# Random-feature attention and a feed-forward layer on one core: attention's matmuls in plain float32, each head on half of the array

## The chip, the cores and the metric

The kernel runs on one core of a Trainium2 chip. The metric is the device time of one execution in microseconds; less is better. The core's engines work side by side, each with its own queue of instructions: TensorE (PE; its weight loads are listed apart as PEld), VectorE (DVE), ScalarE (ACT), GpSimd (POOL) and SyncE (SP), which issues most of the transfers.

## The reference

There are 8 batches, 8 heads, 576 tokens, a head size of 64, 128 features and a hidden size of 2048, all in float32.

```python
scale = 1.0 / np.sqrt(np.sqrt(D))
q_s, k_s = q * scale, k * scale
def phi(x):
    h = x @ omega.T - sum(x * x) / 2          # 64 -> 128 features
    h = h - max(h over features)
    return exp(h) / sqrt(128)
q_p, k_p = phi(q_s), phi(k_s)
kv = einsum('bhsm,bhsd->bhmd', k_p, v)        # sums over the tokens
z = sum(k_p over the tokens)
out = (q_p @ kv) / (q_p @ z + 1e-6)
x = out as (8 * 576, 512)
h = x @ w_in                                  # 512 -> 2048
result = (h - tanh(h)) @ w_out                # 2048 -> 512
```

The term sum(x * x) / 2 and the factor 1 / sqrt(128) fall away: the maximum is subtracted, and the quotient has the rest on both sides.

## The kernel before

**Layout.** Queries and keys lie transposed in memory, two heads in one tensor: partitions 0 to 63 hold the head dimensions of head 0 of a pair, partitions 64 to 127 those of head 1. There are four pairs (`c`). The 4608 tokens are cut into 18 chunks (`ch`) of 256 for queries and for the feed-forward part; keys go by batch (`b`) of 576 tokens, four tiles of 128 and a last one of 64. A pair's two last tiles of 64 share one tile.

**Units.** `k_unit(b, c)` makes, for a batch and a pair, the sums kv and z; `q_unit(ch, c)` makes the attention of a chunk and a pair and leaves it in `xh` and `xl` (`x_split`), the operand of the feed-forward part. Both are generators; `tick` starts new ones by a table of start times (`start`) and carries each one a step further. Between steps come the feed-forward steps `ffn_h` (hidden, tanh) and `ffn_out` (output sums), with a `beat` of attention after each. The instructions' order on each engine follows from the order of issue and from the scheduler's own timing model (`schedule_with_timeline_sim=True`).

**Two formats.** A plain float32 matmul is one call and shows as two pairs of weight load and matmul in the trace. The feed-forward part, and attention from batch 2 and chunk 3 on, split each operand into a high and a low part of the format float32r, which shows as one load and one matmul for each call.

**First stage (`native=True`), batches 0 and 1 and chunks 0 to 2.** Attention is in plain float32 over all 128 rows. `features_f` (L153) multiplies a token tile of both heads with `om_bd`, omega for both heads on a block diagonal, 256 columns. The values carry a column of ones (width E = 66), so the sum over the tokens gives kv and z at once (L201, L205); the last, shared tile is spread over block diagonals `kd` and `vd` by POOL copies (L184, L185). z is brought to all partitions by two transposes (L221). kv is held for both heads on a block diagonal `kvf`, so the numerators of two heads add up in one accumulator (L374). In this stage the feed-forward weights are also fetched and decoded (`fetch`, `decode`: ACT, DVE and POOL work on 16 weight blocks), and the first feed-forward steps begin.

**Steady stage (`native=False`), the rest.** `split_rows` (ACT L75, DVE L129 and L130) puts the high part of a head in 64 rows and its low part in the other 64. `features` (L132) multiplies with `om2`, omega's high and low part side by side, 256 columns; ACT copies one half (L143), DVE adds the other and finds the minimum (L146), ACT takes the exponentials (L150). `k_single` (L227) splits features and values (POOL L250 and L258, DVE L249 and L259), sums them on TensorE (L266), adds up z on POOL (`zsum`, L271 and L272, L289, L290), and brings kv and z into place with two transposes and two multiplications with ones (L302, L304). `q_unit` divides the features by the denominators (DVE L347, L350, L359), transposes them (L366), splits them (ACT L389, DVE L390), multiplies with the split kv (L396, L397), and adds the halves (ACT L400 and L401, DVE L402 and L403).

**PSUM.** Its eight banks have tags (`pj0`, `pj1`, `pk`, `pt`, `po0`, `po1`, `h0`, `h1`). `h0` and `h1` belong to the hidden layer, `po0` and `po1` to the output. `mode` says which tags projections (`pj`), sums (`pk`) and transposes and numerators (`pt`) rotate through. A two-head projection lies in one bank.

**Order around the change.** SP issues the loads, in the first stage in program order (`chain=True`), and each engine works through its queue in order.

Of the kernel before, what the change touches and what calls it, by code (L numbers as in the profile page):

```python
# [8 lines left out]
F32 = mybir.dt.float32  # L9
# [10 lines left out]
P = 128  # L20
# [3 lines left out]
TC = 256  # L24
# [7 lines left out]
def favor_attention_ffn(ctx: ExitStack, tc: tile.TileContext, qT, kT, va, vt, omT, w, out):  # L32
# [63 lines left out]
    omf = a0.tile([P, M], F32, name="omf")  # L96
# [7 lines left out]
    om2 = om.rearrange("p a m -> p (a m)")  # L104

    om_bd = a0.tile([P, 2, M], F32, name="om_bd")
    nc.gpsimd.memset(om_bd, 0.0)
    nc.gpsimd.tensor_scalar(om_bd[0:D, 0], omf[0:D], -SCALE, 1.0, op0=ALU.mult, op1=ALU.mult)
    nc.gpsimd.tensor_scalar(om_bd[D:P, 1], omf[D:P], -SCALE, 1.0, op0=ALU.mult, op1=ALU.mult)

    oms = a0.tile([P, M], F32, name="oms")
    nc.gpsimd.tensor_scalar(oms, omf, -SCALE, 1.0, op0=ALU.mult, op1=ALU.mult)

    def kv_tiles(pool, names):

        ts = [(pool.tile([P, 9, E], F32, name=f"v{i}"), pool.tile([P, P], F32, name=f"kd{i}"),
               pool.tile([P, 2, E], F32, name=f"vd{i}")) for i in names]
        for v, kd, vd in ts:
            for x in (kd, vd):
                nc.gpsimd.memset(x, 0.0)  # L120
            nc.gpsimd.memset(v[:, :, D:], 1.0)
        return ts


    def split_rows(x, f):

        copy(mode["hi"], x[0:D, 0, :], f[0:D])
        copy(mode["hi"], x[D:P, 1, :], f[D:P])
        nc.vector.tensor_sub(x[D:P, 0, :], f[0:D], x[0:D, 0, :].bitcast(F32))  # L129
        nc.vector.tensor_sub(x[0:D, 1, :], f[D:P], x[D:P, 1, :].bitcast(F32))  # L130

    def features(lhs, name):  # L132

        n = len(lhs)
        ph = att("phi", [P, 4, M], F32, f"phi_{name}")
        nb = sb.tile([P, 4], F32, tag="nb", name=f"nb_{name}", bufs=12)

        for g in range(0, n, 2):
            m = min(2, n - g)
            pj = ps.tile([P, 2, 2 * M], F32, tag=bank("pj"), name=f"pj_{name}_{g}")  # L140
            for i in range(m):
                nc.tensor.matmul(pj[:, i], lhs[g + i], om2, start=True, stop=True)  # L142
            nc.scalar.copy(ph[:, g : g + m], pj[:, :m, M:])  # L143
            for i in range(m):
                j = g + i
                nc.vector.tensor_tensor_reduce(  # L146
                    ph[:, j], pj[:, i, :M], ph[:, j], scale=-SCALE, scalar=3.0e38,
                    op0=ALU.add, op1=ALU.min, accum_out=nb[:, j : j + 1])
        for j in range(n):
            nc.scalar.activation(ph[:, j], ph[:, j], AF.Exp, bias=nb[:, j : j + 1], scale=-1.0)  # L150
        return ph

    def features_f(f, toks, name):  # L153

        n = 2 * len(toks)
        ph = att("phi", [P, 4, M], F32, f"phi_{name}")
        nb = sb.tile([P, 4], F32, tag="nb", name=f"nb_{name}", bufs=12)
        pj = ps.tile([P, 4, M], F32, tag=bank("pj"), name=f"pj_{name}")
        for i, (a, b) in enumerate(toks):
            nc.tensor.matmul(pj[:, 2 * i : 2 * i + 2].rearrange("p a m -> p (a m)"), f[:, a:b],  # L160
                             om_bd.rearrange("p a m -> p (a m)"), start=True, stop=True)
# [505 lines left out]
```

## Time and profile before

| | |
|---|---|
| time, median of 3 runs | 1067.35 us (1067.0 to 1067.55) |
| profiled execution, span from first to last instruction | 1065.4 us |
| PE busy | 1041.8 us (98%), 6760 records |
| DVE busy | 855.5 us (80%) |
| ACT busy | 696.4 us (65%) |
| POOL busy | 325.9 us (31%) |
| DMA | 55.90 MB, 52 GB/s over the span |

For the profiled execution the profile gives the span and no other time of its own; the three runs' times lie 1.6 to 2.2 us above it, for what comes ahead of the first and after the last instruction. A row of a group reads: line, engine, operation, tile written <- tiles read, shape, number of records, then busy time in us and mean length of one in ns, then idle time of the engine ahead of them and what ended it. A matmul's record is longer than the distance to the next one's start, since matmuls are pipelined.

### The profile page before, as it was taken

How to read it: one execution, taken by the hardware profiler on the slowest of the kernel's cores; microseconds unless marked ns; L12 is line 12 of the kernel's file. 1: busy time of each engine (PE TensorE's matmuls, PEld its weight loads, DVE VectorE, ACT ScalarE, POOL GpSimd, SP SyncE). 2: the span in 40 equal slices, each digit the busy share in tenths (PEclk: the TensorE clock that was granted, in tenths of full speed). 3: DMA queues.
4: the chain of work that ended last, by engine and by line, in shares of the span. 5: the costliest groups of instructions: out<-in, count | busy, mean ns of one | idle time of the engine just before them, and what ended most of it. 6: DMA issues, size and time to landing. Idle time of an engine off the chain costs nothing.

```text
span 1065.4 us, 20130 instructions
## 1 busy us (share of the span) xinstructions
PE 1041.8 (98%) x6760; PEld 945.6 (89%) x6760; DVE 855.5 (80%) x2910; ACT 696.4 (65%) x1773; POOL 325.9 (31%) x553
## 2 busy tenths in 40 slices
PE   7988999999999999999999999999999999999998
PEld 7766888999889999999999998999999999999997
DVE  5999995889998886789889878998888887666522
ACT  6997655777677665577777766677767675555422
POOL 4634541344333420133333344333333331000000
PEclk9999999999999999999999999999999999999999
DMA  8750401111111110011111111111101110000000
GB/s 265 237 213 3 187 1 42 53 39 46 31 53 33 54 33 31 11 53 33 53 34 53 34 37 44 33 53 29 47 25 49 33 37 11 30 16 21 1 21 21
DMA packets 35528, 55.90 MB, mean 52 GB/s; under 512 B 12256, under 2 KB 21600, under 8 KB 33376
## 3 DMA queue, kind: packets, MB, share of 16 engines
q1 hardware_dynamic: 35344, 54.57, 16.3%
q8 instruction: 54, 0.88, 0.3%
q14 instruction: 50, 0.41, 0.1%
q10 hardware_dynamic: 80, 0.03, 0.0%
HBM read 45.15 MB, written 9.44 MB: 51 GB/s over the span
## 4 chain that ended last, share of the span: by engine, by line
PE 61%; DVE 2%; ACT 1%; POOL 1%; issue 0%; DVEq 0%; POOLq 0%
PE h L471 26%; PE po L489 8%; PE po L490 8%; PE po L491 8%; PE pj_q L142 2%; PE pk L266 2%; PE pt L366 2%; PE pn L397 1%; PE pn L396 1%; PE pj_kb L142 1%; PE pj_ka L142 1%; PE pk L304 0%; PE pk L302 0%; DVE junk L347 0%; POOL khl L250 0%
## 5 line engine op out<-in xcount | busy, mean ns | idle before, releaser
L471 PE MATMUL h<-xh,w 128*128 128x256 f32 (+1 forms) x2176 | 450.1, 290 | 3.9 <-DVE g L476 2.1
L471 PEld LDWEIGHTS h<-xh,w 128*128 128x128 f32 x2176 | 354.8, 190 | 14.7 <-DVE g L476 3.2
L471 PE MATMUL h<-xl,w 128*128 128x256 f32 (+1 forms) x1088 | 315.8, 290 | 0.0
L489 PE MATMUL po<-w,gh 128*128 128x512 f32 x544 | 213.7, 393 | 0.0
L490 PE MATMUL po<-w,gh 128*128 128x512 f32 x544 | 213.3, 392 | 0.0
L471 PEld LDWEIGHTS h<-xl,w 128*128 128x128 f32 x1088 | 206.9, 190 | 6.0
L491 PE MATMUL po<-w,gl 128*128 128x512 f32 x544 | 209.2, 391 | 0.0
L477 ACT CAST gh<-g 128x512 fp32r<-128x512 f32 x144 | 89.4, 621 | 92.8 <-DVE g L476 91.3
L475 ACT ACTIVATE g<-h 128x512 f32<-128x512 f32 x144 | 85.4, 593 | 95.0 <-PE h L471 82.7
L476 DVE TENSOR_TENSOR g<-h,g 128x512 f32<-128x512 f32 x144 | 98.7, 686 | 57.8 <-ACT g L475 56.6
L478 DVE TENSOR_TENSOR gl<-g,gh 128x512 fp32r<-128x512 f32 x144 | 108.2, 751 | 34.9 <-ACT gh L477 33.1
L491 PEld LDWEIGHTS po<-w,gl 128*128 128x128 f32 x544 | 102.1, 188 | 20.5
L489 PEld LDWEIGHTS po<-w,gh 128*128 128x128 f32 x544 | 102.5, 188 | 16.2
L490 PEld LDWEIGHTS po<-w,gh 128*128 128x128 f32 x544 | 102.5, 188 | 15.3
L347 DVE CUSTOM_DVE_ANT_0 junk<-phi_q,zb 128x128 f32<-128x128 f32 (+1 forms) x320 | 98.5, 309 | 14.4 <-ACT phi_q L150 0.5
L150 ACT ACTIVATE phi_q<-phi_q,nb_q 128x128 f32<-128x128 f32 x240 | 79.6, 392 | 6.8 <-DVE nb_q L146 6.7
L442 POOL TENSOR_SCALAR a<-a 128x1024 f32<-128x1024 f32 x14 | 58.7, 4194 | 54.6 <-ACT a L438 37.2
L250 POOL TENSOR_TENSOR khl<-phi_ka,khl 128x256 fp32r<-128x256 f32 x48 | 37.9, 796 | 121.6 <-DVE khl L249 92.5
L258 POOL CAST vhl<-v 128x128 fp32r<-128x128 f32 (+1 forms) x144 | 45.8, 319 | 91.9 <-PE pk L266 71.5
L390 DVE TENSOR_TENSOR ql<-pt,qh 128x512 fp32r<-128x512 f32 x60 | 41.1, 685 | 32.3 <-ACT qh L389 31.8
L146 DVE CUSTOM_DVE_ANT_0 phi_q<-pj_q,phi_q 128x128 f32<-128x128 f32 x240 | 56.0, 283 | 2.3 <-ACT phi_q L143 2.2
L389 ACT CAST qh<-pt 128x512 fp32r<-128x512 f32 x60 | 34.9, 581 | 32.9 <-PE pt L366 32.6
(152 smaller groups left out, 1938.2 us busy)
## 6 DMA issues: line engine op xcount, KB each, us to landing
raw<-w SPq DMA_DIRECT2D x16, 1024.0 KB, 7.3
kf<-kT SPq DMA_DIRECT2D x32, 288.0 KB, 2.9
qf<-qT SPq DMA_DIRECT2D x72, 128.0 KB, 2.1
out<-o SPq DMA_DIRECT2D x36, 256.0 KB, 2.0
v<-vt SPq DMA_DIRECT2D x24, 288.0 KB, 2.8
v<-va SPq DMA_DIRECT2D x8, 288.0 KB, 5.9
omf<-omT ACTq DMA_DIRECT2D x1, 32.0 KB, 2.2
omf<-omT SPq DMA_DIRECT2D x1, 32.0 KB, 2.4
```

The costliest lines, as they stand in the source:

```text
L146: nc.vector.tensor_tensor_reduce(ph[:, j], pj[:, i, :M], ph[:, j], scale=-SCALE, scalar=3.0e38, op0=ALU.add, op1=ALU.min, accum_out=nb[:, ...
L150: nc.scalar.activation(ph[:, j], ph[:, j], AF.Exp, bias=nb[:, j : j + 1], scale=-1.0)
L347: nc.vector.tensor_tensor_reduce(bank("junk")[r], ph[r, i], kvs[b, c][1][r, h], scale=1.0, scalar=EPS, op0=ALU.mult, op1=ALU.add, accum_ou ...
L442: engine.tensor_scalar(a.bitcast(F32), a.bitcast(F32), 2.0**-15, 122879.9921875, op0=ALU.max, op1=ALU.min)
L471: nc.tensor.matmul(o, w_, x, start=i == 0, stop=i == len(prods) - 1)
L475: nc.scalar.activation(g, p, AF.Tanh)
L476: nc.vector.tensor_sub(g, p, g)
L477: nc.scalar.copy(gh, g)
L478: nc.vector.tensor_sub(gl, g, gh.bitcast(F32))
L489: nc.tensor.matmul(po[t], h, wt[f][:, 0, DM:], start=first, stop=False)
L490: nc.tensor.matmul(po[t], h, wt[f][:, 1, DM:], start=False, stop=False)
L491: nc.tensor.matmul(po[t], l, wt[f][:, 0, DM:], start=False, stop=last)
```

## The change

One code path serves all batches and chunks, in plain float32. There is no split of attention's operands any more and no block diagonal.

- *Projections* (`features`, new): each head is one matmul of 64 rows (its 64 partitions) by 128 token columns against omega's 128 columns; the two heads stand in the two row halves of the array and write to two PSUM banks, in the order tile 0 head 0, tile 0 head 1, tile 1 head 0, tile 1 head 1. The minimum is taken by one reduce per head over two tiles, the exponentials read PSUM.
- *Last tile of the keys*: two matmuls of 64 by 64, one per head, into the two halves of one bank. No `kd`, no `vd`.
- *Sums of kv*: the values are now the stationary operand (64 columns per head) and the features stream (128 columns): head 0 in the column half that ends in partitions 0 to 63, head 1 in the other, alternating, five pairs. The result is copied and transposed once.
- *z*: added up on POOL for all batches (`zt`, `zs`), split into high and low part (`zhl`) and multiplied with ones, as the steady stage did before.
- *Numerators*: each head's kv has 64 columns, one matmul per head and piece, side by side by columns, straight into the layout that `x_split` reads.
- *Banks*: one list `at` for all attention tiles, first 8 banks, then 6, then 2, then 4.
- *Start times* of the units shift by 2 to 3 beats, as units have fewer steps. The values of all batches use one layout (`va`) and `load`.

```diff
-    om = const.tile([P, 2, M], F32R, name="om")
-    nc.vector.tensor_copy(om[:, 0], omf)
-    nc.vector.tensor_sub(om[:, 1], omf, om[:, 0].bitcast(F32))
+    om = const.tile([P, M], F32, name="om")
+    nc.vector.tensor_scalar(om, omf, -SCALE, 1.0, op0=ALU.mult, op1=ALU.mult)
...
+    def bank_tile(shape, name):
+        return ps.tile(shape, F32, tag=bank("at"), name=name)
+
+    def features(f, toks, name):
+
+        ph = att("phi", [P, 2, 2, M], F32, f"phi_{name}")
+        nb = sb.tile([P, 2, 2], F32, tag="nb", name=f"nb_{name}", bufs=12)
+        pj = [bank_tile([P, 2, M], f"pj_{name}_{h}") for h in range(2)]
+        for t, (a, e) in enumerate(toks):
+            for h in range(2):
+                r = slice(D * h, D * h + D)
+                nc.tensor.matmul(pj[h][:, t], f[r, a:e], om[r], start=True, stop=True)
+        for h in range(2):
+            nc.vector.tensor_reduce(nb[:, h], pj[h], axis=AX.X, op=ALU.min)
+            for t in range(2):
+                nc.scalar.activation(ph[:, h, t], pj[h][:, t], AF.Exp, bias=nb[:, h, t : t + 1], scale=-1.0)
         return ph
...
     def k_unit(b, c):
...
         phs = []
         for t in range(0, 4, 2):
-            phs.append(features_f(f, [(t * P, t * P + P), (t * P + P, t * P + 2 * P)], f"k{t}_{n}"))
+            phs.append(features(f, [(t * P, t * P + P), (t * P + P, t * P + 2 * P)], f"k{t}_{n}"))
             yield
...
-        nc.tensor.matmul(pj, kd, oms, start=True, stop=True)
+        for r in rows:
+            nc.tensor.matmul(pj[r], f[r, 4 * P : S], om[r], start=True, stop=True)
         nc.vector.tensor_reduce(nb[:, 0:1], pj, axis=AX.X, op=ALU.min)
         nc.scalar.activation(ph, pj, AF.Exp, bias=nb[:, 0:1], scale=-1.0)
...
+        nc.gpsimd.tensor_add(zt, phs[0], phs[1])
+        nc.gpsimd.tensor_add(zs, zt[:, :, 0], zt[:, :, 1])
+        for h, r in enumerate(rows):
+            nc.gpsimd.tensor_add(zs[r, h], zs[r, h], ph[r])
+        zhl = att("zhl", [P, 2, 2, M], F32R, f"zhl_{n}")
         nc.vector.tensor_copy(zhl[:, 0], zs)
         nc.gpsimd.tensor_sub(zhl[:, 1], zs, zhl[:, 0].bitcast(F32))
+        yield
+        yield
+        pk = bank_tile([P, M], f"pk_{n}")
+        for t in range(5):
+            for h, r in enumerate(rows):
+                if t < 4:
+                    nc.tensor.matmul(pk[r], v[:, 5 * h + t], phs[t // 2][:, h, t % 2], start=t == 0, stop=False)
+                else:
+                    nc.tensor.matmul(pk[r], v[r, 4], ph[r], start=False, stop=True)
+        c1 = att("c1", [P, M], F32, f"c1_{n}")
+        nc.scalar.copy(c1, pk)
+        yield
+        pz = bank_tile([P, 4, M], f"pz_{n}")
+        nc.tensor.transpose(pz[:, 0], c1, ident)
         for i in range(2):
+            nc.tensor.matmul(pz[:, 2:4].rearrange("p h m -> p (h m)"), ones,
                              zhl[:, i].rearrange("p h m -> p (h m)"), start=i == 0, stop=i == 1)
+        w = att("kvw0" if b == 0 else "kvw", [P, 2, D], F32, f"kvw_{n}")
+        nc.scalar.copy(w.rearrange("p h d -> p (h d)"), pz[:, 0])
+        zb = att("zb0" if b == 0 else "zb", [P, 2, M], F32, f"zb_{n}")
+        nc.scalar.copy(zb, pz[:, 2:4])
+        kvs[b, c] = (w, zb)
...
     def q_unit(ch, c):
...
+        qf = att("qt", [P, 2, TC], F32, f"qt_{n}")
+        nc.scalar.copy(qf.rearrange("p h t -> p (h t)"), pt)
+        yield
+        pn = bank_tile([P, TC], f"pn_{n}")
+        for b, s, e in pieces:
+            for h in range(2):
+                nc.tensor.matmul(pn[D * h : D * h + D, s:e], kvs[b, c][0][:, h], qf[:, h, s:e], start=True, stop=True)
...
-            k = [28,30,33,35][c] if ch == 3 else [42,45,48,52][c] if ch == 4 else 16 * (ch - 1) - 6 + 4 * c
+            k = [30, 32, 35, 37][c] if ch == 3 else [44, 47, 50, 54][c] if ch == 4 else 16 * (ch - 1) - 4 + 4 * c
...
-            k = 28 + 5 * c if b == 2 else 16 * (need[b] - 1) - 25 + 8 * c
+            k = 28 + 5 * c if b == 2 else 16 * (need[b] - 1) - 22 + 8 * c
```

More of the change, by code (lines that the diff above doesn't have):

```diff
@@ L132, in features @@
[L132 to L150, printed above, removed]
-        return ph
@@ L153, in features_f @@
[L153 to L161, printed above, removed]
-        nc.vector.tensor_reduce(nb[:, :n], pj[:, :n], axis=AX.X, op=ALU.min)
-        for j in range(n):
-            nc.scalar.activation(ph[:, j], pj[:, j], AF.Exp, bias=nb[:, j : j + 1], scale=-1.0)
-        return ph
@@ L172, in k_unit @@
         n = f"{b}_{c}"
[L173 to L177 removed]
         f = att("kf", [P, S], F32, f"kf_{n}")
         load(f, kT[c, :, b * S : (b + 1) * S])
[L180 to L185 removed]
+        v = att("v", [P, 9, D], F32, f"v_{n}")
+        load(v, va[b, c])
         yield
@@ L525, in favor_attention_ffn @@
     mode.update(
[L526 to L534 removed]
+        chain=True, kvw=(sb, 7), zb=(sb, 6), kvw0=(a0, 4), zb0=(a0, 4), phi=(a0, 8), ph5=(a0, 2), qf=(a0, 2),
+        qt=(a0, 2), kf=(a0, 3), v=(a0, 3), zt=(a0, 1), zs=(a0, 2), zhl=(a0, 2), c1=(a0, 2), native=True,
+        junk=[junk, a0.tile([P, M], F32, name="junk1")], norm=[nc.vector, nc.scalar], h=["h0", "h1"],
+        at=["pj0", "pj1", "po0", "po1", "pk", "pt", "h0", "h1"])
     start = {}
```

248 lines of the change are left out of this document (32 added, 216 removed).

## The prediction

> **What bounds the kernel now.** I read the page first (engines, slices, the chain that ended last), then the waits of TensorE, then stretches of time.
>
> ```profile
> span 1065.4 us, 20130 instructions
> PE 1041.8 (98%) x6760; PEld 945.6 (89%) x6760; DVE 855.5 (80%) x2910; ACT 696.4 (65%) x1773; POOL 325.9 (31%) x553
> PE   7988999999999999999999999999999999999998
> ...
> PEclk9999999999999999999999999999999999999999
> ...
> PE 61%; DVE 2%; ACT 1%; POOL 1%; issue 0%; DVEq 0%; POOLq 0%
> ...
> 0.00:100.00 100.00, 84.04 (x455) 69.77 (x456) 88.23 (x253) 81.54 (x225) 45.80 (x66) 0.98 0.60 190
> 100.00:240.00 140.00, 140.00 (x784) 122.25 (x783) 117.38 (x290) 93.72 (x190) 56.20 (x60) 1.00 0.17 62
> 240.00:320.00 80.00, 77.49 (x522) 69.79 (x521) 74.02 (x272) 57.02 (x155) 31.52 (x62) 1.00 0.15 43
> 320.00:1065.00 745.00, 740.24 (x5006) 683.79 (x5005) 575.92 (x2097) 464.12 (x1205) 192.34 (x366) 1.00 0.11 33
> ```
>
> The last four rows give length, then busy PE, PEld, DVE, ACT, POOL, the granted clock and DMA. From 100 us on TensorE is full at clock 1.00, but for 2.5 us in the third stretch. So in the steady part (24 key units of batches 2 to 7, 60 query units) the time is the sum of TensorE's slots, and work taken from DVE, ACT or POOL there is worth only those small holes. In the first 100 us (8 key and 12 query units) no engine is alone the bound: DVE is 88% busy, PE 84%, ACT 82%.
>
> What a slot costs is the distance between starts; a record's length has a tail in it that the next matmul overlaps.
>
> ```profile
> 1013.49 2.87 PE h L471 x24
> ...
> 43.13 1.90 PE L160 MATMUL pj_q<-om_bd,qf 128*128 128x256 f32 x8
> 44.86 0.39 PE L205 MATMUL pk<-vd,ph 128*128 128x132 f32 x2
> ...
> 53.91 0.39 PE L194 MATMUL pj<-oms,kd 128*128 128x128 f32 x2
> 54.13 1.03 PE L374 MATMUL pn<-qt,kvf 128*128 128x256 f32 x4
> ...
> 58.46 1.90 PE L201 MATMUL pk<-v,phi_k 128*128 128x66 f32 x16
> ...
> 601.77 0.60 PE L366 MATMUL pt<-ident,phi_q 128*128 128x128 f32 x4
> 602.13 0.36 PE L471 MATMUL h<-xl,w 128*128 128x256 f32 x1
> 602.33 0.40 PE L471 MATMUL h<-xh,w 128*128 128x256 f32 x2
> ```
>
> Split-format (float32r) matmuls of 256 columns: 2.87/24 = 0.12 us. Plain float32 runs as two records per call: 256 columns take (44.86 - 43.13)/8 = 0.216 us per record, 128 columns (54.13 - 53.91)/2 = 0.11. With 66 columns the record does not get cheaper: (1.90 less a tail-long record of 0.28)/15 = 0.108. So about 0.11 us is the floor that a load of 128 weight columns sets. A float32 transpose is one record of 0.11: four and one matmul of 0.12 fill 602.33 - 601.77 = 0.56.
>
> **The change part by part.** First what TensorE does before, by group (records, busy time, mean length).
>
> ```profile
> L142 PE MATMUL pj_q<-om,qx 128*128 128x256 f32 x240 | 41.6, 282 | 0.0
> L142 PE MATMUL pj_ka<-om,kx 128*128 128x256 f32 x96 | 17.4, 282 | 0.0
> L142 PE MATMUL pj_km<-om,kx 128*128 128x256 f32 x24 | 6.9, 286 | 0.0
> L266 PE MATMUL pk<-khl,vhl 128*128 128x256 f32 x240 | 49.4, 288 | 0.8 <-POOL khl L250 0.8
> L302 PE MATMUL pk<-ident,c 128*128 128x128 f32 x48 | 9.3, 275 | 0.8 <-DVE c L299 0.7
> L396 PE MATMUL pn<-qh,kvw 128*128 128x256 f32 x80 | 21.2, 285 | 0.0
> L396 PE MATMUL pn<-qh,kvw 128*128 128x128 f32 x32 | 7.2, 265 | 0.4 <-DVE ql L390 0.4
> L396 PE MATMUL pn<-qh,kvw 128*128 128x192 f32 x24 | 7.4, 309 | 0.0
> L160 PE MATMUL pj_k<-om_bd,kf 128*128 128x256 f32 x64 | 16.5, 390 | 2.4 <-DMA kf<-kT 1.0 <-POOL om_bd L109 0.7 <-ACT phi_q L164 0.7
> L160 PE MATMUL pj_q<-om_bd,qf 128*128 128x256 f32 x48 | 13.6, 413 | 0.3 <-ACT phi_q L164 0.2
> L201 PE MATMUL pk<-v,phi_k 128*128 128x66 f32 x128 | 18.9, 282 | 3.7 <-ACT phi_k L164 3.2
> L374 PE MATMUL pn<-qt,kvf 128*128 128x256 f32 x32 | 8.7, 395 | 3.3 <-ACT qt L369 3.3
> ```
>
> Steady key unit, before: 4 + 4 + 1 = 9 projections (the other four-tile group equals pj_ka) and 240/24 = 10 sums at 0.12, two transposes at 0.11: 2.50 us. (The two ones-matmuls stay.) Query unit: four projections 0.48; numerators 0.60, from 160 records of 256 columns at 0.12 and 160 narrower ones at the 0.11 floor over 60 units: 1.08 us. The four transposes stay.
>
> After, every call works on half the array, so this trace holds nothing like it. Bounds: the two heads' halves wholly side by side, or one after the other. No row here is near, as every record is 128*128. I take side by side, because head 0 and head 1 use different rows (projections) or columns (sums, numerators) and, row-wise, different banks; but with one reservation that the trace does show. Each float32 call is two records in order, so the stream is A1 A2 B1 B2 (two heads A, B): B1 cannot begin before A2, which waits for A1. Overlap is then A2 with B1, B2 with the next A1: n pairs take 2n + 1 slots, one lost per group.
>
> The page "TensorE: Matmul & The Clock Gate", Part 3, of the Trainium skill says the same of order (matmuls start and end strictly in program order) and gives 3.07 times the speed for four row strips; no run here shows it so far.
>
> Key unit after: two groups of two pairs at 5 x 0.11, the last tile 3 x 0.11, sums of five pairs 11 x 0.11, one transpose 0.11: 1.10 + 0.33 + 1.21 + 0.11 = 2.75, so +0.25; x24 = **+6**. Query unit: 5 x 0.11 = 0.55; numerators in 40 units (80 records before, two per unit) 3 x 0.216 = 0.65, in the 20 that straddle batches about 0.55 to 0.60: 0.63 on average; 1.18 in all, +0.10; x60 = **+6**. Steady sum +12.
>
> First 100 us, key unit before: 8 x 0.216 + 16 x 0.11 + last tile 2 x 0.11, its sum 2 x 0.11, two transposes of z 0.22 = 4.15; after 2.75 + two ones-matmuls 0.24 = 2.99: -1.16, x8 = -9. Query: 4 x 0.216 + numerators about 0.94 = 1.80 before, 1.18 after, x12 = -7. Together -16 us of TensorE work, in a stretch with 16 us of holes already, where others are as full:
>
> ```profile
> PE pn L374 <- ACT qt L369: 3.3, 4, 1.5
> PE pk L201 <- ACT phi_k L164: 3.2, 3, 2.0
> PE h L471 <- DVE g L476: 2.1, 2, 1.1
> ...
> L162 DVE TENSOR_REDUCE nb_k<-pj_k 128x4 f32<-128x512 f32 x16 | 10.8, 681 | 5.0 <-PE pj_k L160 5.0
> L195 DVE TENSOR_REDUCE nb<-pj 128x1 f32<-128x128 f32 x8 | 2.2, 275 | 0.6 <-PE pj L194 0.6
> L271 POOL TENSOR_TENSOR zt<-phi_ka 128x256 f32<-128x256 f32 x24 | 19.7, 823 | 106.0 <-ACT phi_ka L150 101.3 <-PE pk L302 2.8 <-DVE nb_km L146 1.9
> L296 POOL TENSOR_TENSOR zhl<-zs,zhl 128x256 fp32r<-128x256 f32 x24 | 18.0, 750 | 9.9 <-DVE zhl L295 9.9
> L442 POOL TENSOR_SCALAR a<-a 128x1024 f32<-128x1024 f32 x14 | 58.7, 4194 | 54.6 <-ACT a L438 37.2 <-DVE dn L347 11.0 <-DVE a L445 4.6
> ```
>
> DVE gains nothing there: one reduce of 512 (0.68) becomes two of 256, between 0.275 and 0.68 each, say 0.41, so +0.14 x 28 = 4 us, and a cast of zhl per key unit is added. ACT keeps its exponentials. POOL takes over the sums of z: zt of 512 is 2 x 0.82, zs of 256 0.82, two half adds about 0.6 each, zhl 0.75: some 4.4 us per key unit, and it stands in one queue with decodes of 4.2 us, so z, and with it the denominators, can come 4 us later. Against 16 us of work saved I take **-5** (ends: -16, all of it on the path; +4, a late z per start and nothing saved).
>
> Elsewhere: the steady part loses the operand splits on ACT, DVE and POOL. They hide under a full TensorE; what shows are the 2.5 us of holes of the third stretch: **-3** with the last ones after it. Exponentials now read PSUM, so banks are held over a reduce and two exponentials; units are spread over 745 us and four banks rotate, so I cost that at nothing. If that cover fails, it is about 1.2 us per features call. The value loads keep their size, and DMA at 0.11 hides them; on SP's queue they now follow the same load order as keys.
>
> Sum: 1065.4 + 12 - 5 - 3 = 1069.4 for the span. The median of the runs shown, 1067.35, lies 2 us above the span. Forecast **1072 us**, its own range 1060 to 1085.
>
> **Rivals.**
> 1. No overlap: halves run one after the other. Key unit: 40 records at 0.11 and a transpose = 4.51, +2.0, x24 = +48; query 8 x 0.11 + 0.87 = 1.75, +0.67, x60 = +40; first stretch +5, holes -3: 1065.4 + 90 + 2 = **1157**. For it: nothing here shows two matmuls at once. Against: separate rows, columns and banks.
> 2. Row halves overlap their streams, but weight loads of 128 columns go one at a time at 0.11. Then projections gain nothing (key 2.20 + 1.21 + 0.11 = 3.52, +1.02, x24 = +24; query 0.88 + 0.63 = 1.51, +0.43, x60 = +26), sums and numerators load 64 columns and do gain. First stretch -3, holes -3: **1111**. For it: the floor of 0.11 at 66 columns is a load's, not a stream's.
> 3. Each change of the array's division costs. Per key unit 8 changes, per query unit 4: 432 in the steady part. Price: from nothing (float32 transposes inside float32r matmuls, the 0.56 us above, cost nothing extra) to the tail that then can't be overlapped, 0.282 - 0.12 = 0.16 us. The full price gives 1072 + 70 = 1142, half of it **1107**. It decides from 0.03 us on. The Trainium skill, "TensorEngine Tiling (Array Packing)", Key Properties, has the rule that speaks for this: a change of tiling mode, not just of tile, drains the engine; by it the time would be that of this rival, and no row here shows a change of mode.
> 4. The other side: the two lanes run free of each other, 2n slots and no loss. Key unit 0.88 + 0.22 + 1.10 + 0.11 = 2.31, -0.19, x24 = -4.5; query 0.44 + 0.44 = 0.88, -0.20, x60 = -12; first stretch -7, holes -3: 1065.4 - 26.5 + 2 = **1041**. For it: loads already run ahead (PEld is 89% busy beside a full PE). Against: records of one engine start in order in every row here. It is faster as soon as fewer than half the groups lose their slot.
>
> **How the numbers follow.** Forecast 0.33, rival 4 0.20, rival 3 0.20, rival 1 0.14, rival 2 0.11, others 0.02. A measurement of this kernel tells about 0.2% (2 us) from no change. Inside the forecast's own range I put 0.11 below 1065, 0.06 within, 0.16 above. Faster 0.20 + 0.11 + 0.01 = 0.32; same 0.07; slower 0.61. The range takes in rival 4 and, above, rivals 2 and 3 with full price; left out are rival 1 and the ends of 3 and 4, near 0.2: 1040 to 1145.
>
> **What would show it.** Starts of head 0's second record and head 1's first within some ns, and 5 slots of 0.11 for a features group: the forecast. Four slots: rival 4. Eight: rival 1, or rival 2 if only in projections while sums of five pairs take 11. A hole of 0.03 to 0.16 us before and after each group: rival 3. In the first 100 us, TensorE's busy share must fall by about 16 us of work and the first pure stretch begin near 95 us. It would be wrong if the pairs are torn apart by feed-forward matmuls between the heads, or if PE waits for banks (rows naming exponentials of phi) grow past a few us.

## The result, and the profile after

The changed kernel takes 1177.66 us (median of four, 1176.49 to 1181.05) against 1067.34 us before: ratio 1.1043 [1.1025, 1.1061]. The forecast was 1072 us, range 1040 to 1145. "Slower" was right, the size was not.

The page of the kernel after: engines, slices, granted clock, and the chain that ended last.

```profile
span 1174.5 us, 19401 instructions
PE 1141.9 (97%) x7632; PEld 944.7 (80%) x7632; DVE 594.1 (51%) x1577; ACT 498.5 (42%) x1217; POOL 182.9 (16%) x180
...
PE   6878899999999999999999999999999999999998
...
PEclk8557999999999999999999999999999999999999
...
PE 91%; DVE 5%; POOL 2%; ACT 1%; issue 1%; DMA 0%; SPq 0%; ACTq 0%; POOLq 0%
```

DVE lost 261 us and ACT 198 us of work, and TensorE still sets the end. Two things are new: TensorE's own busy time is 100 us longer, and the clock row has a dip to 5 in the first slices. The same stretches as in the prediction (length, then busy PE, PEld, DVE, ACT, POOL, granted clock, DMA):

```profile
0.00:100.00 100.00, 78.83 (x446) 57.07 (x446) 80.53 (x192) 64.14 (x168) 53.28 (x45) 0.64 0.40 140
100.00:240.00 140.00, 132.27 (x703) 103.52 (x703) 99.48 (x198) 77.50 (x152) 44.98 (x20) 0.96 0.24 91
240.00:320.00 80.00, 80.00 (x575) 66.45 (x575) 37.51 (x112) 32.54 (x86) 10.99 (x15) 1.00 0.14 40
320.00:1174.00 854.00, 850.85 (x5915) 717.62 (x5913) 376.61 (x1076) 324.32 (x813) 73.60 (x100) 1.00 0.10 30
...
211.00:1174.00 963.00, 959.85 (x6685) 807.92 (x6683) 427.09 (x1228) 370.57 (x935) 88.29 (x120) 1.00 0.10 32
```

A fixed point in the program parts the loss: the feed-forward part of chunk 2, the first with 256 columns after the passes of 512. In the timelines (start in us, length of a row, instructions) that is here, first before (the second of the two records in the row at 172.09), then after:

```profile
172.09 0.51 PE L471 MATMUL h<-xh,w 128*128 128x512 f32 x2
172.43 0.40 PE L142 MATMUL pj_q<-om,qx 128*128 128x256 f32 x2
```

```profile
210.77 0.39 PE L321 MATMUL pt<-w,gl 128*128 128x512 f32 x1
210.99 0.28 PE L301 MATMUL h<-xh,w 128*128 128x256 f32 x1
```

The start comes 39 us later (172 to 211). Twelve output matmuls (12 x 0.23 = 2.7 us) that stand behind this point before stand ahead of it after, so the parting is good to some 3 us. From there to the end it was 893 us:

```profile
172.00:1065.00 893.00, 885.73 (x5985) 816.40 (x5983) 706.14 (x2576) 570.91 (x1488) 248.83 (x478) 1.00 0.12 35
```

and is now 963.5: 71 us more, with TensorE full at clock 1.00 in both. So there are two losses, and the experiments take them one at a time.

### The profile page after: what moved, and what is told of

It reads as the page before. It is cut to its first block, busy times and chain, and to the rows that moved or that the text cites. A ratio compares the mean times of both kernels' runs of the same rounds, so it can differ in the third digit from the quotient of the medians.

```text
span 1174.5 us, 19401 instructions
## 1 busy us (share of the span) xinstructions
PE 1141.9 (97%) x7632; PEld 944.7 (80%) x7632; DVE 594.1 (51%) x1577; ACT 498.5 (42%) x1217; POOL 182.9 (16%) x180
## 4 chain that ended last, share of the span: by engine, by line
PE 91%; DVE 5%; POOL 2%; ACT 1%; issue 1%; DMA 0%; SPq 0%; ACTq 0%; POOLq 0%
PE h L301 37%; PE po L319 11%; PE po L321 11%; PE po L320 11%; PE pj_q L115 5%; PE pn L226 3%; PE pj_k L115 3%; PE pt L219 3%; PE pk L159 2%; POOL a L272 1%; DVE a L275 1%; PE pj L141 1%; PE pk L161 1%; DVE junk L199 1%; DVE m L278 1%
## 5 line engine op out<-in xcount | busy, mean ns | idle before, releaser
L301 PEld LDWEIGHTS h<-xh,w 128*128 128x128 f32 x2176 | 349.2, 189 | 31.8 <-issue 10.7
L146 POOL TENSOR_TENSOR zt<-phi_k,phi_k 128x512 f32<-128x512 f32 x32 | 41.5, 1296 | 675.2 <-ACT phi_k L119 675.1
L308 DVE TENSOR_TENSOR gl<-g,gh 128x512 fp32r<-128x512 f32 x144 | 101.1, 702 | 75.7 <-ACT gh L307 70.5
L119 ACT ACTIVATE phi_q<-pj_q,nb_q 128x128 f32<-128x128 f32 x288 | 86.0, 369 | 103.3 <-DVE nb_q L117 103.3
L199 DVE CUSTOM_DVE_ANT_0 junk<-phi_q,zb 128x128 f32<-128x128 f32 (+1 forms) x320 | 104.4, 330 | 34.1 <-ACT phi_q L119 11.0
L119 ACT ACTIVATE phi_k<-pj_k,nb_k 128x128 f32<-128x128 f32 x256 | 74.3, 373 | 59.1 <-DVE nb_k L117 58.3
L117 DVE TENSOR_REDUCE nb_q<-pj_q 128x2 f32<-128x256 f32 x144 | 57.1, 420 | 65.8 <-PE pj_q L115 65.5
L115 PEld LDWEIGHTS pj_q<-om,qf 64*128 64x128 f32 x576 | 61.9, 201 | 34.5 <-issue 24.0
L115 PE MATMUL pj_q<-om,qf 64*128 64x128 f32 x576 | 86.7, 318 | 2.3 <-ACT phi_q L119 1.0
L117 DVE TENSOR_REDUCE nb_k<-pj_k 128x2 f32<-128x256 f32 x128 | 49.0, 417 | 31.1 <-PE pj_k L115 30.9
```

Source lines behind the costliest of these rows:

```text
L115: nc.tensor.matmul(pj[h][:, t], f[r, a:e], om[r], start=True, stop=True)
L117: nc.vector.tensor_reduce(nb[:, h], pj[h], axis=AX.X, op=ALU.min)
L119: nc.scalar.activation(ph[:, h, t], pj[h][:, t], AF.Exp, bias=nb[:, h, t : t + 1], scale=-1.0)
L199: nc.vector.tensor_tensor_reduce(bank("junk")[r], ph[r, h, t], kvs[b, c][1][r, h], scale=1.0, scalar=EPS, op0=ALU.mult, op1=ALU.add, accum ...
L301: nc.tensor.matmul(o, w_, x, start=i == 0, stop=i == len(prods) - 1)
L308: nc.vector.tensor_sub(gl, g, gh.bitcast(F32))
```

## Which stage loses how much: e1 and e2

Each kernel has one stage as before and the other as after.

```diff
# e1_first_full: after, batches 0, 1 and chunks 0 to 2 with before's code
+    om_bd = a0.tile([P, 2, M], F32, name="om_bd")   # features_f, kd, vd, kvf as before
...
# e2_first_halves: before, with after's features, sums, z and numerators there
-    nc.tensor.matmul(pj[...], f[:, a:b], om_bd[...], start=True, stop=True)
+    nc.tensor.matmul(pj[h][:, t], f[r, a:e], omn[r], start=True, stop=True)
```

> First stage (batches 0 and 1, chunks 0 to 2) as before, on the full array with block diagonals; everything after it on halves as in the changed kernel. In the two traces the first stage lost 39 us (chunk 2 of the feed-forward part starts at 211 us, before at 172) and the rest 71 us (964 against 893 us). Theory, two separate losses: 1067 + 71 = 1138 us, within 6, with a granted clock of 1.0 after 25 us. Rival, one loss: the steady stage runs late only because the first one left it a backlog: under 1090 us.

> First stage on halves as in the changed kernel, the rest in the split format on the full array as before. Theory, two separate losses: 1067 + 39 = 1106 us, within 6, and the clock granted at 0.5 for some 70 to 80 us of the first 115. Rival, one loss that starts in the first stage: 1150 us or more. Rival, all of it in the steady stage: 1067 us.

Measured: e1 1145.64 us (ratio 1.0737 [1.0718, 1.0755]), e2 1106.72 us (1.0373 [1.0355, 1.0392]). Chunk 2 starts at 179 us in e1 and at 208 us in e2. From there to the end of the span e1 needs 964.5 us (after 963.5), e2 894.5 us (before 893). So the length of the steady stage does not depend on how the first is done: 71 us belong to the steady stage, some 39 to the first. e2 came out as expected; e1 missed by 8 us, 6 of which lie ahead of chunk 2.

## The steady stage: what a change of the array's division costs

A change of division is the step from matmuls on one shape of the array to matmuls on another, for instance from the full array to two row halves. Here is the rival that charges each change, against the forecast (a lost slot in each group) and against halves that do not overlap. The timeline of the kernel after, in the steady stage (64*128 are row halves, 128*64 column halves, 128*128 the full array):

```profile
702.05 0.72 PE L115 MATMUL pj_q<-om,qf 64*128 64x128 f32 x8
702.71 0.39 PE L301 MATMUL h<-xl,w 128*128 128x256 f32 x1
...
706.88 0.39 PE L319 MATMUL po<-w,gh 128*128 128x512 f32 x1
707.11 0.39 PE L320 MATMUL po<-w,gh 128*128 128x512 f32 x1
707.33 0.39 PE L321 MATMUL po<-w,gl 128*128 128x512 f32 x1
707.65 1.09 PE L159 MATMUL pk<-phi_k,v 128*64 128x128 f32 x16
708.68 0.44 PE L161 MATMUL pk<-ph,v 64*64 64x128 f32 x4
709.04 0.39 PE L301 MATMUL h<-xh,w 128*128 128x256 f32 x1
709.26 0.29 PE L301 MATMUL h<-xl,w 128*128 128x256 f32 x1
709.39 0.40 PE L301 MATMUL h<-xh,w 128*128 128x256 f32 x2
...
715.29 0.39 PE L321 MATMUL po<-w,gl 128*128 128x512 f32 x1
715.61 0.71 PE L115 MATMUL pj_q<-om,qf 64*128 64x128 f32 x4
716.24 0.39 PE L301 MATMUL h<-xh,w 128*128 128x256 f32 x1
...
717.03 0.49 PE L115 MATMUL pj_q<-om,qf 64*128 64x128 f32 x2
717.44 0.66 PE L226 MATMUL pn<-qt,kvw 128*64 128x64 f32 x8
718.04 0.48 PE L115 MATMUL pj_q<-om,qf 64*128 64x128 f32 x2
718.45 0.50 PE L301 MATMUL h<-xh,w 128*128 128x256 f32 x2
```

Read the starts. Sixteen records of the sums take 708.68 - 707.65 = 1.03 us, 0.064 each, with the change to 64*64 already in it: well below the 0.11 that was the floor for a record of the full array. A whole features group of eight row halves takes 702.71 - 702.05 = 0.66 us: four slots of 0.11, and 0.2 for the change out of rows and a first load that nothing covers. The halves do run side by side. Ahead of them, 707.65 - 707.33 = 0.32 us, where the same matmul takes 0.23 when another of the full array follows (707.11 to 707.33): 0.09 us for the change itself. Behind them, the first matmul of the full array holds 709.26 - 709.04 = 0.22 us instead of 0.12: its weights were not loaded ahead across the change (the record of its load starts at 709.04 too, and that of the next load at 709.15, 0.11 ahead of its matmul). And from 715.61 to 718.45 one features group of eight records stands in three pieces, 4, 2 and 2, with other work between: it is torn, and its records then run one by one and no longer in pairs.

The price was then measured by itself: before's kernel with extra matmuls at the head of each of the 144 feed-forward steps `ffn_h`, into a bank that the step then overwrites.

```diff
         p = ps.tile([P, 2, TC], F32, tag=bank("h"), name=f"h_{ch}_{s}")
+        nc.tensor.matmul(p[:, 0, 0:P], ident, ident, start=True, stop=True)   # p1_full
...
+        for _ in range(1):                            # p2_cols1; range(4): p3_cols4
+            for r in (slice(0, D), slice(D, P)):
+                nc.tensor.matmul(p[r, 0, 0:P], ident[:, r], ident, start=True, stop=True)
```

> The kernel before with one extra full-array float32 matmul of 128 columns ahead of each of the 144 hidden steps, its result overwritten. Both theories: 144 x 0.22 = +32 us at most; a few us less, as the first stage has holes: 1092 to 1099 us.

> As the kernel with one extra full matmul per hidden step, but the extra is one pair of column halves, which fills the same 0.22 us. Theory, each change of the array's division costs about 0.09 us of drain and a weight load that nothing hides (0.05 us for 64 columns, 0.11 us for 128): 0.09 + 0.05 + 0.09 + 0.11 = 0.34 us a step, x144 = 49 us over the full one, 1140 to 1150 us. Rival, the price in the changed kernel comes from torn pairs and waits, not from the change of division itself: no more than 8 us over the full one. Rival, the tail of a matmul only (0.16 us per change): +46 us, which this run does not tell from the theory, but its records do.

> As the kernel with one extra pair of column halves per hidden step (1148 us), but four pairs. Theory, pairs run wholly side by side and the price of a change is paid once a group: 3 x 0.218 x 144 = +94 us, 1242, within 6. Rival, one slot is lost between pairs or the halves run one after the other: +140 to +188 us.

Measured: p1 1101.05 us (1.032 [1.0301, 1.0338]), p2 1148.25 us (1.0763 [1.0746, 1.078]), p3 1291.89 us (1.21 [1.2082, 1.2118]). p1's call and p2's pair both fill two slots of 0.11, so p2 less p1 is in the main two changes of division: 47.2 / 144 = 0.328 us a group, 0.164 a change. It is not quite clean, since 15 of the 144 pairs are torn into two runs in p2's trace. Its timeline shows where the price lies for a whole pair:

```profile
700.79 0.39 PE L493 MATMUL po<-w,gh 128*128 128x512 f32 x1
701.02 0.39 PE L494 MATMUL po<-w,gl 128*128 128x512 f32 x1
701.34 0.44 PE L466 MATMUL h<-ident 128*64 128x128 f32 x4
701.70 0.39 PE L474 MATMUL h<-xh,w 128*128 128x256 f32 x1
701.93 0.28 PE L474 MATMUL h<-xl,w 128*128 128x256 f32 x1
```

0.32 instead of 0.23 into the division; 0.36 instead of 0.22 inside (0.09 for the change out, 0.05 for the first load of 64 columns); 0.23 instead of 0.12 for the first full matmul. That is 0.09 + 0.14 + 0.11 = 0.34 for a whole pair, near the 0.328 from the times; with the torn pairs the times should have given some more, and that difference is not explained.

p3 was expected to add three more pairs at two slots each, 94 us, and added 143.6. Its trace has the reason:

```profile
701.52 0.87 PE L466 MATMUL h<-ident 128*64 128x128 f32 x10
702.32 0.50 PE L266 MATMUL pk<-khl,vhl 128*128 128x256 f32 x2
...
709.55 1.09 PE L466 MATMUL h<-ident 128*64 128x128 f32 x16
710.57 0.39 PE L474 MATMUL h<-xh,w 128*128 128x256 f32 x1
```

A whole group is one run of 16 records in 1.02 us; only 67 of the 144 are whole. The rest were torn (10 and 6 records, 14 and 2, and so on) by the order that the scheduler chose, and each tear pays two more changes. Against p2 that is 111 runs more (at 0.33 us, 37 us) and 268 more records alone in the array (at half a slot, 0.0545 us, 15 us): 52 us for the 50 that were not expected. By the time alone the rival on record, pairs that overlap less or not at all (+140 to +188), would fit as well; the 1.02 us of a whole group rule it out. So long groups do not save themselves: they must also stay together.

The sum for the steady stage, from counts over the trace of the kernel after. There are 478 changes of division, 190 to the full array, 156 to row halves, 84 to column halves, 48 to 64*64. At 0.092 each, 44 us; an uncovered load of 128 columns at 0.107 for 346 of them, 37 us; of 64 columns at 0.05 for 132, 7 us: 88 us. Of the 107 features groups from here on 29 are torn into 78 runs; all 232 of their records run alone in the array, 0.0545 us each, 13 us. Together 101 us; summed directly (tiled runs 168.5 us against 104.0 for their slots, and 34.9 around full matmuls) it is 99. Against it stand the slots of attention, 156.8 us before and 138.5 after. -18 + 99 = +81 is 10 more than the 71 measured: 4 of these are idle time, which went from 893.00 - 885.73 = 7.3 to 963.00 - 959.85 = 3.2 in the rows above, 3 are the twelve output matmuls ahead of the fixed point, and the rest is not placed.

## Undoing the row halves: e10

The projections of both stages go back to the full array in plain float32 (block diagonal, two matmuls of 256 columns, one bank, one reduce). They then cost twice the slots, but change no division.

```diff
-            for h in range(2):
-                r = slice(D * h, D * h + D)
-                nc.tensor.matmul(pj[h][:, t], f[r, a:e], om[r], start=True, stop=True)
+            nc.tensor.matmul(pj[:, t].rearrange("p h m -> p (h m)"), f[:, a:e],
+                             om_bd.rearrange("p h m -> p (h m)"), start=True, stop=True)
...
```

> The changed kernel with the projections of two token tiles back on the full array with a block diagonal (both stages; two matmuls of 256 columns, 4 x 0.216 = 0.86 us a group, no change of division, one bank and one reduce). The last key tile, sums and numerators stay on halves. In the changed kernel's trace a whole row group takes 0.65 us, and 0.09 ahead of it and 0.11 behind it are lost too, 0.85 us; but 39 of 108 steady groups are torn into two or three runs, at 1.05 us of runs and some 0.4 of changes. Theory, changes of division plus torn heads: the torn ones' excess goes, 39 x 0.6 = 23 us, 1178 to 1155, within 6, and the first stage gets its clock back, up to 10 less. Rival, the pairs are worth their half time: TensorE's work doubles for projections, 1178 + 108 x 0.3 = 1210.

Measured: 1152.36 us (1.0793 [1.0775, 1.0811]), 25 us faster than after. From chunk 2 on it needs 948 us, 15.6 us less than after, though every projection holds the array for longer: the changes and tears cost more than halving the slots saved. The expectation counts 39 torn groups; the trace has 29, which at its own 0.6 us each are 17 us, near the 15.6. The other 9 to 10 us lie ahead of chunk 2.

## The first stage: the clock, and POOL's sums

The forecast had -5 us here, and it became +39. Three causes were tried: TensorE at half clock, the z sums that moved to POOL, and the number of buffers.

**The clock.** In the kernel after TensorE was granted 0.50 from 18 to 90 us (before, only from 21.7 to 25.1). The only edit of e12 is row halves, with the two banks and two reduces that they need, in the 28 projection groups of before's first stage (late in it the second bank is one that the sums use too):

```diff
-            nc.tensor.matmul(pj[...], f[:, a:b], om_bd[...], start=True, stop=True)
+            for h in range(2):
+                r = slice(D * h, D * h + D)
+                nc.tensor.matmul(pj[h][:, t], f[r, a:b], oms[r], start=True, stop=True)
```

> The kernel before, with only the projections of two token tiles in the first stage on row halves (28 groups); last key tile, sums, z, numerators and the whole steady stage as before. Theory, work on row halves does not hold the clock up and delays the first stage by itself: the clock is at 0.5 for over 30 us of the first 110 and the time 5 to 12 us above 1067. Rival, the clock falls only where TensorE waits for POOL's sums: no more than 7 us at 0.5 and the time within 3 us of 1067 (28 groups at 0.85 us take as long as at 0.86 us before).

Measured: 1106.22 us (1.0345 [1.0315, 1.0375]), +39 us where 5 to 12 had been expected, and chunk 2 at 208 us. Its stretch, and that of the kernel after:

```profile
8.00:93.00 85.00, 81.10 (x315) 65.86 (x314) 58.72 (x164) 53.75 (x143) 29.53 (x33) 0.50 0.45 143
```

```profile
18.00:90.00 72.00, 56.66 (x259) 40.10 (x260) 66.88 (x153) 46.95 (x117) 40.43 (x26) 0.50 0.31 106
```

In this execution of e12 TensorE is 95% busy for 85 us at clock 0.50, and DVE, which was the fullest engine before, has 58.7 of 85 us. Followed back by the releasers from the decode of the eleventh weight block, the chain was about 115 us long before, 72 of it on DVE and 27 on TensorE; in e12 it is about 150 us, 105 of it on TensorE.

That looks as if the half clock cost the 39 us, but the other executions speak against it. The four of e12 had a mean granted clock of 0.959, 0.989, 0.991 and 0.981; if all that is missing was time at 0.50, these are an estimated 90, 24, 20 and 42 us of it. They took 1106.69, 1100.35, 1105.74 and 1106.78 us. Only the first was traced, and with a fifth of its time at half clock the third is 1 us faster. 20 us at half clock hold back at most 10 us of TensorE's work, so the half clock does not carry most of the loss. The trace shows one more thing: more than half of the row groups are torn, since 132 of their 224 records run alone, and the stage has 78 changes of division, 39 ways in and out. At the steady stage's prices that is an estimate of 28 x 0.44 + 39 x 0.40 + 132 x 0.0545 = 35 us of TensorE time at full clock, where the groups took 28 x 0.86 = 24 before. What makes the rest of the 39 us (the second bank that a group holds, the second reduce, the order that the scheduler made of it) is open.

Does half-array work let the clock fall, or idle time? e3 and e4 add the same multiplications to each of the 28 first-stage groups of the kernel after, once for the full array and once as row halves; e13 adds a quarter of e3's. The results go to unused columns of the same banks.

```diff
+            for i in range(4):                                     # e3_warm_full
+                nc.tensor.matmul(pj[i % 2][:, 2 + i // 2], ident, omf, start=True, stop=True)
...
+            for i in range(4):                                     # e4_warm_halves
+                for h in range(2):
+                    r = slice(D * h, D * h + D)
+                    nc.tensor.matmul(pj[h][:, 2 + i % 2], ident[r], omf[r], start=True, stop=True)
...
+            nc.tensor.matmul(pj[1][:, 2], ident, omf, start=True, stop=True)    # e13_warm1
```

> The changed kernel with four extra full-array float32 matmuls of 128 columns (0.88 us at full clock) after each projection group of the first stage, 28 groups, 25 us of added TensorE work; their results are not used. Theory, the half clock makes the first stage late: the clock stays at 1.0 after some 25 us and the time falls by 30 to 44 us, to 1134 to 1148. Rival, the load queue and the chain over DVE and POOL make it late and the clock is a bystander: the clock may return, but the time stays within 10 us of 1178 or rises by up to 25.

> As the kernel with extra full-array matmuls, but the same 0.88 us of extra work per group as four pairs of half-array matmuls. Theory A, matmuls on half of the array do not hold the clock up: it stays at 0.5 for over 60 us and the time is 1178 or more, up to 1200. Theory B, the clock falls because TensorE is idle too often, whatever the shape: clock and time as with the full-array ones, 1134 to 1148.

> The changed kernel with one extra full-array float32 matmul of 128 columns (0.22 us at full clock) per projection group of the first stage, 6 us of added work in all, its result not used. Theory, the half clock itself costs time: it is at 0.5 for under 60 us of the first 120 (82 in the changed kernel) and the time falls by 5 us or more, under 1173. Rival, the clock only follows the waits and costs nothing: the time stays within 4 us of 1178 even if the clock comes back.

Measured: e3 1179.08 us (1.1067 [1.1003, 1.1131]), e4 1201.79 us (1.1303 [1.123, 1.1376]), e13 1183.19 us (1.1085 [1.1068, 1.1101]). The stretches of e3, then of e4:

```profile
20.00:60.00 40.00, 36.13 (x237) 27.39 (x235) 35.95 (x78) 27.62 (x69) 28.43 (x18) 0.91 0.28 89
60.00:100.00 40.00, 36.17 (x189) 26.19 (x189) 30.07 (x88) 24.62 (x63) 16.89 (x13) 0.74 0.27 93
```

```profile
60.00:80.00 20.00, 20.00 (x90) 16.94 (x90) 4.24 (x17) 5.87 (x18) 2.00 (x2) 0.50 0.18 61
80.00:104.00 24.00, 24.00 (x119) 19.94 (x119) 13.97 (x37) 12.44 (x31) 11.12 (x7) 0.50 0.29 97
```

In e4 TensorE has not a hole for 44 us and is still at 0.50; 4.0 of the 44 us are full-array work. In e3 it is only 90% busy and has 0.91 and 0.74, and 34.9 of its 72 busy us are full-array work. So idle time alone does not explain the clock. That half-array work does is not shown either: in e12's 85 us at 0.50 more than half of the busy time, 46.2 of 81.1 us, is full-array work, and p4 (below), which has no halves at all, is at 0.50 for 31 us. What decides the clock stays open. The Trainium skill, "TensorE: Matmul & The Clock Gate", Part 1, lets about 3.4 us of busy time release the throttle; 44 busy us that stay at 0.50 differ from that, and here the measurement decides. What the clock alone is worth in the kernel after stays unmeasured: e3's extra work fills the time that the faster clock frees (36 of 40 us busy), and e13's is too little to lift the clock (0.50 for 79 us). Nor is e4 less e3 a price of the clock, since 398 of e4's 680 row records run alone and so hold TensorE for longer. In e3 the time does go with the clock: its four executions, with means of 0.974, 0.985, 0.990 and 0.993, took 1190.90, 1181.18, 1176.98 and 1173.99 us.

**POOL's z sums.** p4 adds to before the four additions per key unit of the first stage and uses their result nowhere. e5 is the kernel after with z summed by full-array matmuls with ones in the first stage; e11 is e10 with the same.

```diff
+        nc.gpsimd.tensor_add(zt, phs[0], phs[1])                      # p4_pool
+        nc.gpsimd.tensor_add(zs, zt[:, 0:2], zt[:, 2:4])
+        for h in range(2):
+            r = slice(D * h, D * h + D)
+            nc.gpsimd.tensor_add(zs[r, h], zs[r, h], ph[r])
...
+        for t in range(4):                                            # e5, e11
+            nc.tensor.matmul(pz[:, 2:4], ones_f, phs[t // 2][:, :, t % 2], start=t == 0, stop=False)
+        nc.tensor.matmul(pz[:, 2], top, ph, start=False, stop=False)
+        nc.tensor.matmul(pz[:, 3], bot, ph, start=False, stop=True)
```

> The kernel before, with POOL's four additions for z (one of 512, one of 256, two of half the partitions) after each of the 8 key units of the first stage; their result is not used. Theory, POOL's additions on float32 slow DVE's work on the same memory: DVE's first decode step goes from 0.69 to over 1.0 us in the mean of the first 110 us, and the time rises by 4 to 15 us, 1071 to 1082. Rival, POOL delays only what waits for its result: nothing waits, DVE stays at 0.69 and the time within 2 us of 1067.

> The changed kernel, but in the first stage z is summed and brought to all partitions by TensorE (full-array float32 matmuls with ones) and no longer by POOL, DVE and the two ones-matmuls. The kernel with extra full-array matmuls got most of the clock back (0.985 for 0.965) and was not faster (1179 us), so the clock alone is not the cause. Theory, POOL's sums of z make the first stage late (they slow DVE's decodes: 1.21 us for 0.69 us before, and queue with POOL's decodes): 1178 less 20 to 35 us, 1143 to 1158. Rival, the load queue: within 8 us of 1178.

> As the kernel with projections back on the full array, and in the first stage z is summed by TensorE instead of POOL. Theory, POOL's sums cost the first stage some 12 us (1165 for 1178 us with this part alone) and add up with the projections: 12 below the kernel with projections on the full array, and DVE's first decode step (1.21 to 1.28 us in the changed kernel) at 0.69. Rival, both take away the same first-stage loss: within 4 us of that kernel.

Measured: p4 1086.95 us (1.0182 [1.0167, 1.0198]), some 19 us slower than before, where 4 to 15 had been expected; e5 1165.17 us (1.0927 [1.0907, 1.0948]), 12.5 faster than after; e11 1138.37 us (1.0662 [1.0646, 1.0678]), 14.0 faster than e10. POOL's additions, by group, in p4 in the first 130 us:

```profile
L449 POOL TENSOR_SCALAR a<-a 128x1024 f32<-128x1024 f32 x9 | 35.6, 3958 | 31.4 <-ACT a L445 18.8 <-DVE dn L354 12.3
L199 POOL TENSOR_TENSOR zt<-phi_k,phi_k 128x512 f32<-128x512 f32 x8 | 10.9, 1361 | 10.0 <-ACT phi_k L164 9.6
L203 POOL TENSOR_TENSOR zs<-zs,ph 64x128 f32<-64x128 f32 x16 | 9.5, 593 | 1.0
L200 POOL TENSOR_TENSOR zs<-zt 128x256 f32<-128x256 f32 x8 | 9.4, 1170 | 0.6
```

10.9 + 9.5 + 9.4 = 30 us in eight key units, 3.7 each, about what the prediction put on them. What it missed is their neighbour. Two of DVE's decode operations in the first 110 us (count, busy us, mean ns), in the order before, after, p4, e5:

```profile
L445 DVE SCALAR_TENSOR_TENSOR a<-raw,a 128x1024 uint32<-128x1024 uint32 x10 | 12.2, 1216 | 0.0
...
L444 DVE TENSOR_SCALAR a<-a 128x1024 uint32<-128x1024 uint32 x10 | 6.9, 687 | 0.1
```

```profile
L275 DVE SCALAR_TENSOR_TENSOR a<-raw,a 128x1024 uint32<-128x1024 uint32 x8 | 12.4, 1555 | 0.1
...
L274 DVE TENSOR_SCALAR a<-a 128x1024 uint32<-128x1024 uint32 x8 | 10.2, 1278 | 1.6 <-POOL a L272 1.5
```

```profile
L452 DVE SCALAR_TENSOR_TENSOR a<-raw,a 128x1024 uint32<-128x1024 uint32 x8 | 10.8, 1347 | 0.0
...
L451 DVE TENSOR_SCALAR a<-a 128x1024 uint32<-128x1024 uint32 x9 | 7.0, 781 | 0.1
```

```profile
L313 DVE SCALAR_TENSOR_TENSOR a<-raw,a 128x1024 uint32<-128x1024 uint32 x9 | 11.0, 1218 | 0.1
...
L312 DVE TENSOR_SCALAR a<-a 128x1024 uint32<-128x1024 uint32 x9 | 6.2, 685 | 2.5 <-POOL a L310 2.5
```

The same operations on the same tiles take 1.28 times (1216 to 1555) and 1.86 times as long (687 to 1278) in the kernel after, and are back at 1218 and 685 once the additions leave POOL. In p4, which has only the additions, they rise less, to 1347 and 781. Summed over all of DVE's instructions of the first 130 us, time above each form's shortest is 9.8 us before, 22.0 after, 19.1 in p4, 6.5 in e5. The Trainium skill, "GPSIMD Engine Reference", section 1, has POOL and VectorE share SBUF interfaces and names contention with some DVE instructions; these rows agree.

The rival is the queue: the decodes on POOL could simply stand behind the sums. In the first 130 us of the kernel after they do not: each starts within 0.5 us of the end of the ACT step that it needs. In p4 three start 1.3 to 3.4 us late, 6.5 us in all. How p4's 19 us divide between that, the longer DVE operations and its 31 us at half clock was not measured.

So POOL's sums alone cost 19 us, e12's edit alone costs 39, and after, which has both, loses 39 too: the costs do not add up, and what they delay is the same. The last four weight blocks are loaded only once the first stage's buffers are free; their transfers are issued at 105 to 107 us before, at 123 to 124 in p4, at 143 to 145 in e12 and at 138 to 141 after. Taking one change back leaves most of the loss: e5 leaves 27 of the 39 us (chunk 2 at 199), e10 leaves 30 (202). With both taken back, e11 starts chunk 2 at 188, with 0.50 granted for only some 10 us: 16 us are still open. What is left in it of the change is the column halves of sums and numerators, the last key tile and the banks; those were not tried apart.

**Buffers.** SP stood 85.1 us behind nine loads of queries that waited for a free `qf` (24.2 us before), and the weights' transfers queue behind these:

```profile
SPq L81 <- PE pj_q L115: 85.1, 9, 17.1
```

```diff
# e6_more_buffers
-... phi=(a0, 8), ph5=(a0, 2), qf=(a0, 2), ... kf=(a0, 3), v=(a0, 3), ...
+... phi=(a0, 8), ph5=(a0, 2), qf=(a0, 6), ... kf=(a0, 4), v=(a0, 4), ...
```

> The changed kernel with more room for loads in the first stage: 6 query buffers for 2, 4 key buffers and 4 value buffers for 3 each, so that the weight blocks behind them in SP's queue are issued earlier (the eighth left at 97 us, at 54 us before the change). Theory, the load queue holds the weights back: 1178 less 20 to 35 us. Rival, the queue waits only since the engines are late (POOL, DVE): weights leave early and the time stays within 8 us of 1178.

Measured: 1179.3 us (1.106 [1.1042, 1.1078]). The eighth weight block left at 46.9 us instead of 97.2, and nothing got faster: the last five left from 140.3 us on. The longest wait of the queue was a sign, not the cause.

## Why the prediction was right or wrong, step by step

- **TensorE bounds the steady part, and work taken from the others is worth only small holes:** right. DVE, ACT and POOL lost 31%, 28% and 44% of their work, and idle TensorE went from 7.3 to 3.2 us; 3 had been set for it.
- **"n pairs take 2n + 1 slots":** wrong. In whole groups a record of one head and one of the other start 6 to 14 ns apart, in the order A1 B1 A2 B2, and n pairs take 2n slots. That is rival 4's count, which gave -16.5 us for the steady part; the slots came out at -18.
- **The change of division, costed at nothing from the float32 transposes inside float32r matmuls:** this is the step that failed. Those rows change the format, not the division (all are 128*128), so they were not near. The runs put 88 us there by count (478 changes), 99 with the torn groups. Rival 3's full price, 0.16 us, is near what p2 measures (0.164), and its count, 432, is near 478, but it took the price from a record's tail, 0.282 - 0.12; that the waits and the uncovered loads come to about the same is luck. By it alone the time would have been 1142; the Trainium skill, "TensorEngine Tiling (Array Packing)", Key Properties, had the rule, that a change of tiling mode drains the engine, and here the drain is 0.09 us and the uncovered load behind it up to 0.107. Against rival 3 I had a row that did not speak to it.
- **Pairs torn apart,** named as what would make it wrong: it happened to 29 of 107 features groups, 13 us and the changes that it adds.
- **Banks held by exponentials that read PSUM, at nothing:** right; TensorE has 3.2 us of idle time in the steady stage for all reasons.
- **First 100 us, -5 with ends -16 and +4:** wrong, +39. This is the second step that failed: the term counted TensorE work saved, 16 us, and a late z, put at 4 us a start. Two edits that it held for gains or for nearly free cost time by themselves: the row halves with their second bank and reduce (39 us alone, e12; torn groups are part of it, the half clock carries the smaller part of it at most, the rest is open) and POOL's additions (some 19 us alone, p4, with 9 us more of DVE's time beside them). Both delay the last weight blocks, a path that the prediction did not follow, and 16 us of the 39 remain with both taken back (e11).
- **Rivals 1 and 2:** both out, by 0.064 us a record in the runs of sums, and by 0.66 us for eight records of 64*128, where eight slots alone would be 0.88.

## What to carry to other kernels

Halves of the array double the rate only inside an unbroken run: going in and out costs 0.34 (columns) to 0.40 us (rows, 0.09 + 0.2 + 0.11), and a pair of 128 columns saves 0.22 (four slots of 0.11 become two), so a group needs two pairs to break even and has to stay whole in the instruction order. Inside a stream of full-array matmuls, short groups of halves lose; before adding them, count the changes of shape in the order that is issued, not in the source. And when an edit moves sums to POOL or fills a stage with half-array work, look at DVE's mean durations and at the granted clock of that stage, since both moved here without a row of the edit itself showing it. Then compare the clock of all executions with their times before a loss is put down to it: in e12 the time hardly followed the clock.

## What was not expected of the hardware

- TensorE was granted 0.50 through 85 us of 95% busy time (e12's traced execution; its others had means of 0.981 to 0.991) and through 44 us of 100% (e4).
- A weight load is not run ahead across a change of division: the first full matmul of 256 columns holds 0.22 us instead of 0.12.
- DVE operations of 128x1024 took up to 1.86 times as long (687 to 1278 ns) in the kernel with POOL's float32 additions, and up to 1.14 times (781 ns) when only the additions were put into the kernel before.
- Two halves' plain float32 records interleave at 6 to 14 ns, so the two records of a call cost no lost slot.
